# Attention and a gated layer on one core: f16 loads of q and k on GpSimd's queue, more seven-product groups, GpSimd sums, and a fixed order

## The chip, the core and the metric

The kernel runs on 1 core of one Trainium2 chip. A core has TensorE (PE; its weight loads are the row PEld), VectorE (DVE), ScalarE (ACT), GpSimd (POOL) and SyncE (SP), each with an instruction queue that runs in order, and 16 DMA engines that all queues share. The metric is device microseconds of one execution. Three runs of the kernel before took 285.19, 287.29 and 288.51 us; their median, 287.29 us, is the time before.

## The reference, cut to what matters

```python
def phi(x, c, s):                                    # c, s: cos and sin by position
    r = np.maximum(x, 0.0)
    return np.concatenate([r * c, r * s], axis=-1)   # 64 -> 128 features
q_p, k_p = phi(q, cos_w, sin_w), phi(k, cos_w, sin_w)
kv  = np.einsum('bhsf,bhsd->bhfd', k_p, v)
num = np.einsum('bhsf,bhfd->bhsd', q_p, kv)
den = np.einsum('bhsf,bhf->bhs', q_p, k_p.sum(axis=2))[..., None] + 1e-06
x = (num / den).transpose(0, 2, 1, 3).reshape(B * S, H * D)   # 4608 x 512
h = x @ w_in                                                  # 512 x 2048
out = (h * np.cos(h)) @ w_out                                 # 2048 x 512
```

There are 8 batches, 8 heads, 576 positions and 64 features a head. All inputs and the output are float32 in memory.

## The kernel before, in words

**Tiling.** A batch has 576 positions: four tiles of 128 and a rest of 64. The rests of all eight batches make one more block of 512 rows, so the second half of the work (from here on, the layers) runs over nine blocks c = 0 to 8 of 512 rows. Matmul inputs are f16, sums are f32 in PSUM.

**Attention of a batch b.** `load` (L420) brings q, k and v as float32 into the tiles `raw` (named qm, km, vm), two DMAs for each, all issued by SP. `prep` (L443) makes the features: max(x, 0) times cos or sin, 20 instructions of 128x512 for a batch (q and k, five tiles, two halves of the features), on ACT (L452) or DVE (L453). `cast_v` (L457) makes v f16, on DVE, ACT or POOL (L468). `kv` (L471) multiplies and copies the result to `kvz`. q is transposed by a DMA on SP (`q_dma`, L518) or, for batches 0 and 1, by PE. `num` (L527) multiplies q by kv; DVE divides (L566, L568). The result x is transposed by a DMA on SP (`x_dma`, L597) or, for batches 0 to 2, by PE with a copy on ACT (`x_pe`, L581).

**Layer 1.** Blocks 0 and 1 are computed plainly (L637). From block 2 on, the 16 column tiles of w_in are taken in four groups. A group is done in one of two ways. `layer1_plain` (L671), four times for a group, makes 4 matmuls of 128x512 (L677), then `gate` (L606): a cosine on ACT (L609) and a product on DVE (L614). `layer1_fast` (L749) does the group with seven block products instead of eight (Strassen's scheme in Winograd's form): 7 steps of 4 matmuls of 128x256 (L780), with one copy from PSUM to PSUM on ACT (`seed`, L663), two copies to `Z` on ACT (L789), two additions on DVE (L793), two gates, and one double gate `out2` (cosine of 128x1024 on ACT, L802; product on DVE, L808). It needs sums of w_in made once for each group (`w_in_sums`, four instructions on DVE, L717) and, for each block, four sums of x on DVE (`layer1_sums`, L738). `FAST1` says how many groups of a block are done in the seven-product way: 3 in blocks 3 to 6, 4 in blocks 7 and 8, none in block 2.

**Layer 2.** Block 0 is plain (L880). Blocks 1 to 8 use seven products (L948), with sums of w_out made once (L904), four sums of the gated tiles per block on DVE (L926, L979), copies out of PSUM on ACT (L663, L959, L967) and additions on DVE (L963). Two output tiles `ost` are stored by SP.

**What sets the order.** Every step of the kernel is given to a list by `Plan.add`, with its engine or a choice of engines, an estimated cost and the data that it reads and writes. `Plan.run` then walks through a model of the engines (`forward`), picks at each point the ready step with the smallest number in a table `KEYS`, and chooses the engine of a step that has several by the estimated end. The steps are emitted in the order of their modelled start; each engine's queue gets its own in that order. So nothing on the chip is reordered: an instruction that waits holds all behind it on its engine.

**The start.** POOL copies one element of k to w_in's tile as soon as k of batch 0 has landed, and so holds back w_in (four DMAs on POOL, L1033: float32 in memory, f16 in SBUF) and, after w_in's first quarter, the first half of w_out. Batch 1's loads are held back by a copy out of w_in's third quarter (`GATE1`, `hold_raw`, L1052).

Of the kernel before, what the change touches and what calls it, by code (L numbers as in the profile page):

```python
# [17 lines left out]
    5824, 5995, 5824, 2967, 2673, 126, 143, -359, -2881, 263, -1072, -2121, 539, -49, 2962,  # L18
    2726, 3623, 3679, 1739, 3937, 2137, -2208, -6512, 4069, -2017, 702, -6077, -768, 703, -754,
    -6331, 8159, 3076, -1894, -5732, 1581, -6769, -1234, -877, -673, -882, -751, -1585, -1235,  # L20
    617, -63, -2524, -424, -626, 4458, 1519, -1459, -1432, 1518, -1601, 1517, -828, -5827,
    -6392, 1404, 4308, -2500, 2020, -1958, -2107, -3266, -4898, 8136, -5552, -8420, -2791,
    -1468, -4655, -1451, -1052, 783, -6576, 2792, -3465, -355, -8421, -3123, 6479, -3015, -6472,
    -1591, -2075, -2619, -2729, -7369, -6796, 3263, 798, -2481, 6480, -2003, -7073, 6781, 423,
    1982, 1241, 120, -9188, 1380, 643, -11779, -6829, 9984, -8175, -7566, 1246, -8162, 512,
    -312, -11302, 511, 10443, -10259, 2437, 605, 4807, 1897, 5905, -9831, -5057, 9984, 2301,
    -5301, 8846, -10101, -6662, 9020, -11634, -568, 7671, 5055, -1712, 6604, 584, 1196, 5001,
    -1672, 2279, 3129, 2596, 3289, 895, 532, -4417, -5551, -4542, 2044, 1687, 2846, 2800, 1902,
    3378, 993, -5427, 6673, -5442, 8455, 6488, 5906, 5871, 7397, -1850, 7157, -1228, 5182, 5994,
    7349, -880, 4039, 6762, 7533, 1736, 4177, 11737, 11954, 7479, 6368, 6930, 8684, 7392, 5307,  # L30
    17180, 16483, 5398, 7497, -1619, 7409, 8721, -161, 1062, -838, 10292, 5065, 5035, 7002,
    2938, 4999, 14973, 16942, 5320, 7491, 5034, 4630, 11782, 14974, 11886, 4631, 7315, 4601,
    4503, -692, -956, 4504, 7814, 2937, 3132, -860, 16897, -3069, -418, 10427, 3570, 3895, 4526,
    811, 1495, 8147, 4216, 8205, 4347, 7685, 6163, 8521, 4575, 8538, 4733, 3460, 8421, 9350,
    4611, 8493, 5428, 5849, 9131, 9146, 7933, 8134, 4534, 8052, 5570, 6030, 5703, 3236, 9273,
    5079, 7033, 7959, -732, 8555, 4350, -5307, 8046, 8768, 11196, 7765, 7621, 12926, 8253, 8411,
    11956, 11554, 8883, 13897, 9078, 9732, 12216, 1417, 8512, 13854, 7780, 9806, 6177, 5415,
    9049, -520, 5974, 11813, -2437, 5998, 8827, 10404, 7711, 13087, 3521, 9257, 1171, 1138,
    4633, 11805, 2569, 2323, 2261, 2582, 5745, 6182, 8706, 9578, 5077, 10082, 8860, -990, 8453,
    8541, 6221, 8499, 9036, 12232, 10067, 9664, 8544, 14012, 6360, 6188, 8015, 4438, -1489,  # L40
    6985, 8390, 5805, 5879, 5943, 6028, 8049, 8537, 10462, 5198, 8396, 8395, 12558, 4688, 9262,
    6122, 9046, 8189, 3466, 1589, 7820, 11893, 7819, 12664, 3857, 3643, 11985, 9433, 9054, 9210,
    8708, 8410, 9843, 8144, 4689, 8846, 8992, 9753, 8959, 11174, 12280, 10511, 11156, 9526,
    5553, 7072, 10317, 10402, 10261, 8357, 10403, 10051, 10267, 14404, 18351, 12204, 11240,
    9232, 9255, 18421, 14144, 12777, 11783, 7045, 11215, 9090, 7849, 7075, 9381, 10740, 5609,
    9483, 3041, 12189, 10009, 6763, 11687, 7171, 11186, 8968, 9229, 5228, 8069, 10107, 13655,
    8182, 10208, 13199, 8613, 9303, 15205, 7902, 9952, 15535, 6395, 9744, 4204, 6896, 8110,
    15935, 5192, 9656, 15578, 5752, 11091, 9533, 7831, 11765, 13714, 4074, 11936, 4217, 2177,
    4612, 7204, 2638, 7978, 7784, 4545, 8636, 6647, 6639, 5918, 8225, 3758, 5656, 6600, 8239,
    8692, 9382, 5468, 10740, 10372, 5666, 8703, 3916, 8802, 9066, 9050, 9298, 9304, 4801, 9527,  # L50
    9521, 8286, 11521, 9621, 9449, 6022, 5622, 9514, 9669, 10572, 6135, 8767, 7485, 8972, 9413,
    9995, 4213, 8900, 10075, 9675, 10273, 6234, 14794, 10195, 8079, 8885, 4804, 11145, 9576,
    11000, 9480, 10532, 11021, 11980, 10074, 11419, 13188, 13339, 10446, 11020, 12065, 12937,
    12270, 12793, 12994, 13467, 14479, 13933, 13146, 11684, 12054, 13603, 13106, 11695, 11512,
    14005, 13771, 13161, 15965, 16177, 16249, 16753, 13045, 12409, 18114, 13650, 12372, 12951,
    11343, 17252, 18836, 11725, 9919, 9604, 12293, 15415, 7956, 11448, 14519, 12454, 13519,
    14769, 15313, 12053, 13106, 13257, 13105, 13291, 11473, 11759, 13416, 11450, 13716, 18849,
    11925, 12834, 16093, 13478, 14576, 16431, 12255, 12362, 15960, 13160, 14519, 15910, 14407,
    11420, 14173, 9926, 10508, 15133, 9344, 13280, 12367, 9947, 9788, 14407, 10518, 12980,
    11697, 11766, 15535, 11429, 11430, 11395, 14648, 15418, 12373, 10069, 8755, 10521, 8003,  # L60
    11441, 13572, 10404, 12329, 17053, 10754, 11091, 10405, 4849, 9215, 7332, 8545, 10442, 9859,
    10283, 8824, 11855, 11042, 10408, 9428, 9240, 10089, 6840, 10015, 11937, 13432, 12329,
    14986, 8570, 13601, 11278, 9846, 10850, 12123, 10120, 9231, 12906, 11502, 11095, 17486,
    13263, 10990, 10503, 12334, 12434, 12727, 10556, 12848, 11321, 12810, 13349, 12759, 11144,
    9468, 12544, 13893, 13417, 10912, 9663, 12457, 8909, 13137, 14576, 14577, 13435, 14151,
    10310, 14092, 13571, 10884, 9832, 16768, 15657, 11596, 15684, 17182, 16270, 13098, 17070,
    15987, 15606, 6694, 19176, 16271, 6282, 21578, 15029, 12700, 14864, 23503, 25176, 13602,
    15549, 15974, 10832, 14466, 16061, 14589, 10209, 12007, 14031, 13538, 17903, 15093, 14046,
    16754, 11592, 18103, 14972, 15838, 14550, 15534, 14971, 15051, 13097, 12823, 12047, 14361,
    15045, 11016, 15607, 13066, 17291, 15370, 14684, 17730, 15344, 15696, 14507, 15369, 21381,  # L70
    12422, 13612, 16306, 16082, 6980, 15110, 25709, 16196, 6566, 16377, 16411, 13784, 6718,
    14056, 16929, 17039, 16412, 6717, 14282, 13875, 16186, 15098, 22414, 15303, 22094, 16880,
    22547, 17762, 13257, 17979, 16921, 14246, 17264, 11458, 9954, 12478, 12363, 11239, 12491,
# [50 lines left out]


class Plan:


    LINK = {"PE": 0.12, "ACT": 0.05, "DVE": 0.05, "POOL": 0.1, "SP": 0.0}


    SHARE, WAKE, LAND = {"HW": 0.40, "SW": 0.56}, {"HW": 1.1, "SW": 1.3}, 1.0
    BUSY = 2.2

# [48 lines left out]
    def forward(self, key):  # L183
# [32 lines left out]
        for n, k in enumerate(left):  # L216
            if not k:
                ask(n)
# [980 lines left out]
```

## Time and profile before

| | |
|---|---|
| three runs, us | 285.19, 287.29, 288.51 (median 287.29) |
| the profiled execution, us | 284.34 |
| its span, first to last instruction, us | 282.3 |
| around the span, us | 2.04 |
| mean granted clock of TensorE | 0.993 |
| busy, us: PE, PEld, DVE, ACT, POOL | 270.5, 219.1, 249.2, 218.0, 19.2 |

All durations come from this one profiled execution. A row of the profile gives the line, engine and operation, output <- input with partitions x elements, how often it ran, the busy time, the mean duration of one in ns, and the idle time of the engine just ahead of it with what ended it. A "window" row gives the busy time of each engine in a stretch of the span. Instructions of one engine overlap a little: eight matmuls of 128x256 (273 ns each in the row) follow one another in 0.87 us on the chain of waits, four of 128x512 in 0.86 us.

### The profile page before, as it was taken

The page shows a single profiled execution, that of the slowest core. Times are in us where ns is not written, and L with a number is a line of the kernel's source. Part 1 is how long each engine was busy: PE and PEld are TensorE (multiplying, and loading weights), DVE is VectorE, ACT ScalarE, POOL GpSimd, SP SyncE. Part 2 cuts the span into 40 slices and gives each one's busy share as a digit, 9 for nine tenths or more (in the row PEclk, how much of TensorE's full clock was granted, in tenths as well). Part 3 has the DMA queues.
Part 4 walks back from the last instruction along what each step waited for, and adds up shares of the span by engine and source line. Part 5 has one row for each costly group of instructions (what it writes and reads, how often), then busy time and mean ns, then how long its engine had stood idle before and what let it go on. Part 6 is the DMA issues. An engine that isn't in the chain of part 4 may idle for free.

```text
span 282.3 us, 6870 instructions
## 1 busy us (share of the span) xinstructions
PE 270.5 (96%) x2715; PEld 219.1 (78%) x2715; DVE 249.2 (88%) x443; ACT 218.0 (77%) x396; POOL 19.2 (7%) x32
## 2 busy tenths in 40 slices
PE   7799988999989999999999999999999999999994
PEld 2668956678967667779787988898788888888883
DVE  2877796999999989998999999999999999997952
ACT  2856698896899998599899999996676675877420
POOL 1440020010000010003003000210000000000000
PEclk9799999999999999999999999999999999999999
DMA  6999999969979999997999899988013100300124
GB/s 204 312 200 222 298 291 267 320 133 285 311 231 235 211 229 293 241 310 161 308 234 268 167 275 270 240 117 251 3 37 116 57 2 0 151 0 2 74 77 149
DMA packets 77599, 53.30 MB, mean 189 GB/s; under 512 B 46080, under 2 KB 75264, under 8 KB 77568
## 3 DMA queue, kind: packets, MB, share of 16 engines
q1 hardware_dynamic: 72608, 48.12, 66.7%
q0 software_dynamic: 4224, 4.19, 9.5%
q10 hardware_dynamic: 736, 0.57, 0.6%
q8 instruction: 21, 0.34, 0.5%
q14 instruction: 10, 0.08, 0.1%
HBM read 36.74 MB, written 9.44 MB: 164 GB/s over the span
## 4 chain that ended last, share of the span: by engine, by line
PE 85%; DVE 5%; DMA 4%; ACT 3%; issue 1%; DVEq 0%
PE M L948 32%; PE M L780 15%; PE M L637 10%; PE M L677 7%; PE TR L780 6%; PE M L880 5%; PE ATT L542 3%; DMA xT<-x 2%; PE ATT L479 2%; DMA qm<-in_q_dram 2%; PE M L509 2%; PE ATT L1022 1%; PE TR L677 1%; DVE x L568 1%; ACT xT L593 1%; ACT KQ L452 1%
## 5 line engine op out<-in xcount | busy, mean ns | idle before, releaser
L609 ACT ACTIVATE ch<-M 128x512 f32<-128x512 f32 x90 | 53.3, 597 | 14.4 <-PE M L637 6.9
L614 DVE TENSOR_TENSOR gT<-M,ch 128x512 f16<-128x512 f32 x84 | 56.7, 685 | 5.0 <-ACT ch L609 4.6
L948 PEld LDWEIGHTS <-gT 128*128 128x128 f16 x560 | 54.0, 98 | 7.6 <-DVE gT L926 0.5
L948 PE MATMUL M<-w_out_sb,gT 128*128 128x256 f16 x448 | 55.9, 273 | 0.0
L452 ACT ACTIVATE KQ<-km,CS 128x512 f16<-128x512 f32 x55 | 37.2, 715 | 0.2 <-DMA km<-in_k_dram 0.2
L452 ACT ACTIVATE KQ<-qm,CS 128x512 f16<-128x512 f32 x47 | 32.3, 721 | 4.5 <-DMA qm<-in_q_dram 4.5
L780 PEld LDWEIGHTS <-w_in_sb 128*128 128x128 f16 x320 | 30.8, 98 | 4.3 <-issue 0.2
L948 PE MATMUL M<-T,S 128*128 128x256 f16 x256 | 32.4, 273 | 0.0
L637 PE MATMUL M<-xT,w_in_sb 128*128 128x256 f16 x256 | 30.2, 273 | 0.1
L677 PE MATMUL M<-xT,w_in_sb 128*128 128x512 f16 x112 | 27.6, 379 | 0.8 <-ACT xT L593 0.8
L948 PEld LDWEIGHTS <-S 128*128 128x128 f16 x256 | 24.7, 98 | 4.0 <-issue 0.2
L637 PEld LDWEIGHTS <-w_in_sb 128*128 128x128 f16 x256 | 24.5, 98 | 3.5 <-issue 0.4
L568 DVE TENSOR_TENSOR x<-ATT,rec 128x512 f16<-128x512 f32 x32 | 22.1, 692 | 2.3
L959 ACT ACTIVATE ost<-M 128x512 f32<-128x512 f32 x24 | 14.1, 593 | 12.1 <-PE M L948 9.3
L780 PEld LDWEIGHTS <-WS 128*128 128x128 f16 x216 | 20.5, 98 | 3.3 <-issue 0.5
L677 PEld LDWEIGHTS <-w_in_sb 128*128 128x128 f16 x128 | 12.2, 98 | 10.8 <-issue 0.9
L453 DVE TENSOR_SCALAR KQ<-qm,CS 128x512 f16<-128x512 f32 x33 | 15.4, 498 | 5.1 <-DMA qm<-in_q_dram 5.1
L468 POOL CAST V<-vm 128x1024 f16<-128x1024 f32 (+1 forms) x11 | 10.7, 1004 | 134.9 <-PE M L948 46.0
L542 PEld LDWEIGHTS <-qT 128*128 128x128 f16 x320 | 15.3, 98 | 4.6 <-issue 1.8
L926 DVE TENSOR_TENSOR S<-gT 128x2048 f16<-128x2048 f16 (+1 forms) x16 | 17.4, 1085 | 0.2
L808 DVE TENSOR_TENSOR gT<-Z,ch 128x1024 f16<-128x1024 f32 x13 | 15.9, 1221 | 0.7 <-ACT ch L802 0.4
L542 PE MATMUL ATT<-kvz,qT 128*128 128x65 f16 x288 | 15.7, 194 | 0.6 <-DVE x L568 0.5
(135 smaller groups left out, 461.3 us busy)
## 6 DMA issues: line engine op xcount, KB each, us to landing
out_dram<-ost SPq DMA_DIRECT2D x33, 256.0 KB, 3.0
qm<-in_q_dram SPq DMA_DIRECT2D x8, 640.0 KB, 5.9
km<-in_k_dram SPq DMA_DIRECT2D x8, 640.0 KB, 5.6
qm<-in_q_dram SPq DMA_DIRECT2D x8, 512.0 KB, 6.2
km<-in_k_dram SPq DMA_DIRECT2D x8, 512.0 KB, 5.7
vm<-in_v_dram SPq DMA_DIRECT2D x6, 640.0 KB, 7.2
vm<-in_v_dram SPq DMA_DIRECT2D x6, 512.0 KB, 6.5
w_in_sb<-in_moe_w_in_dram POOLq DMA_DIRECT2D x4, 512.0 KB, 8.9
```

The lines of the kernel that those rows point to most:

```text
L452: fn = {"ACT": lambda: nc.scalar.activation(out=out_, in_=in_, func=AF.Relu, scale=sc), "DVE": lambda: nc.vector.tensor_scalar(out=out_, i ...
L453: "DVE": lambda: nc.vector.tensor_scalar(out=out_, in0=in_, scalar1=0.0, scalar2=sc, op0=ALU.max, op1=ALU.mult)}
L542: nc.tensor.matmul(bank[hb][:, hh * D1:(hh + 1) * D1], lhsT=a[:, h, :], rhs=z[:, h, :], start=(i == 0), stop=(i == len(parts) - 1))
L568: nc.vector.tensor_tensor(out=split(x16[n][:, hs, :], k), in0=A[:, :, :, 0:D], in1=split(rec[n][:, hs], k).unsqueeze(3).broadcast_to((P, k ...
L609: act(0.5, due, lambda: nc.scalar.activation(out=ch[c], in_=bank, func=AF.Sin, bias=math.pi / 2.0, scale=1.0), [key], [("ch", c)])
L614: dve(0.61, due, lambda: nc.vector.tensor_tensor(out=dst, in0=a, in1=b, op=ALU.mult), [key, ("ch", c), *rd], dkeys)
L637: nc.tensor.matmul(M1[m][:, jj * 2 * P:(jj + 1) * 2 * P], lhsT=w_in_sb[:, cc, j * P:(j + 1) * P], rhs=X[:, cc, ts], start=(cc == 0), stop= ...
L677: nc.tensor.matmul(M, lhsT=w_in_sb[:, cc, j * P:(j + 1) * P], rhs=X[:, cc, :], start=(cc == 0), stop=(cc == NCT - 1))
L780: nc.tensor.matmul(bank[0][:, j * TH:(j + 1) * TH], lhsT=a(cc, j), rhs=b[:, cc, :], start=(first and j == 0 and cc == 0), stop=(last and j ...
L808: dve(1.14, due, lambda: nc.vector.tensor_tensor(out=g4, in0=four(uz), in1=four(cc2), op=ALU.mult), zk + ck, [("g", gi(c), h * JH + j, t) ...
L926: dve(0.07 + 1.07 / NG, due, lambda: nc.vector.tensor_tensor(out=out_[:, sl], in0=a[:, sl], in1=b[:, sl], op=op), rd, wr, port=True)
L948: nc.tensor.matmul(bank[0][:, tt * MH:(tt + 1) * MH], lhsT=a[:, j, tt * P:(tt + 1) * P], rhs=b[:, j, :], start=(first and (apart or tt == ...
```

## The change

- `load`: q and k of batches 2 to 7 go to new f16 tiles `R16`, one for q and one for k (`NK = 1`), by DMAs that POOL issues; float32 in memory, f16 in SBUF. v, and batches 0 and 1, stay as they were. `prep` of those batches reads f16. `clear16` clears the unused rest of the two tiles once, on POOL.
- `FAST1`: all four groups in blocks 2 to 8, that is 28 groups in place of 20. `OWN = 4`: all four groups' sums of w_in have tiles of their own (the fourth used q's transposed tiles before).
- `sums`: the sums of w_in, of x, of the gated tiles and of w_out, and the product of `out2`, may run on DVE or POOL. `copies`: the copies out of PSUM may run on ACT or DVE.
- The float32 tiles of q and k share their memory with the tiles T2 to T4, S2 and S3 of layer 2; the sums that write those wait for batch 1's features. The spare tiles of the last two blocks move to R16, vm and V1.
- Batch 1's loads are held back by w_in's first quarter in place of the third.
- `Plan.run` models nothing any more: an entry of `KEYS` divided by ten is the place of the step in the order, and its last digit names the option (0: only one; 1, 2, 3: first, second, third engine in the order in which the code lists them). There are 1461 entries in place of 1407.

```diff
     def run(self):
         st = self.steps
         assert len(KEYS) == len(st)
-        start, done = self.forward([k / 100 for k in KEYS])
-        for s, a, b in zip(st, start, done):
-            s["start"], s["end"] = a, b
-        return sorted(st, key=lambda s: (s["start"], s["n"]))
...
+        for s, k in zip(st, KEYS):
+            self.pick(s, k % 10)
+            s["at"] = k // 10
+        assert all(st[d]["at"] < s["at"] for s in st for d in s["deps"])
+        return sorted(st, key=lambda s: (s["at"], s["n"]))
+
+    def pick(self, s, i):
+        if i:
+            e = list(s["opts"])[i - 1]
+            s["opts"] = {e: s["opts"][e]}
             s.update(zip(("eng", "occ", "lat", "fn"), s["opts"][e]))
...
-    T2, T3, T4 = [sb(f"T{n}", [P, JH, MH]) for n in range(2, 5)]
-    S2, S3 = [sb(f"S{n}", [P, JH, TH]) for n in (2, 3)]
-    raw = {nm: sb(f"{nm}m", [P, H, NT + 1, D], F32) for nm in "kqv"}
+    TS = sb("TS", [P, 5 * JH * MH])
+    T2, T3, T4, S2, S3 = [TS[:, n * JH * MH:(n + 1) * JH * MH].rearrange("p (j m) -> p j m", j=JH)
+                          for n in range(5)]
+    raw = {nm: TS[:, 2 * n * RAW:2 * (n + 1) * RAW].bitcast(F32).rearrange(
+        "p (h t d) -> p h t d", h=H, t=NT + 1) for n, nm in enumerate("kq")}
+    raw["v"] = sb("vm", [P, H, NT + 1, D], F32)
+    NK = 1
+    R16 = {nm: sb(f"{nm}h", [P, NK, H, NT + 1, D]) for nm in "kq"}
...
-    GATE1 = (w_in_sb[0:2, 0, Dff // 2 + 1:Dff // 2 + 2], [("w_in", 2)])
+    GATE1 = (w_in_sb[0:2, 0, 1:2], [("w_in", 0)])
...
+    def copies(due, cost, out_, in_, rd, wr, hint):
+        either(due, cost, {
+            "ACT": lambda: nc.scalar.activation(out=out_, in_=in_, func=AF.Copy),
+            "DVE": lambda: nc.vector.tensor_copy(out=out_, in_=in_)}, rd, wr, hint, port=False)
+
+    def sums(due, n, out_, in0, in1, op, rd, wr, lazy=None, rate=0.523e-3):
+        def go(q):
+            return lambda: q.tensor_tensor(out=out_, in0=in0, in1=in1, op=op)
+        either(due, {"DVE": 0.07 + n * rate, "POOL": 0.05 + n * 2.15e-3},
+               {"DVE": go(nc.vector), "POOL": go(nc.gpsimd)}, rd, wr, 1, lazy=lazy)
...
     def load(b, nm, due, hs=(slice(0, H),)):
-        m, n = raw[nm], b % 2
+        (m, key), n = staged(b, nm), b % 2
+        cast = m.dtype == F16
+        q = nc.gpsimd if cast else nc.sync
...
+    def clear16():
+        for nm in "kq":
+            pl.add("POOL", 1.2, 1.35, 22, lambda nm=nm: nc.gpsimd.memset(R16[nm][:, :, :, NT, :], 0.0), [],
+                   [x for n in range(NK) for x in hk(f"{nm}h{n}")], port=True)
...
-        out_, in_ = dst[:, t, hs, g, :], raw[nm][:, hs, t, :]
+        m, key = staged(b, nm)
+        out_, in_ = dst[:, t, hs, g, :], m[:, hs, t, :]
...
-        act(0.5, due, lambda: nc.scalar.activation(out=dst[0], in_=bank[0], func=AF.Copy),
-            [bank[1]], [dst[1]])
+        copies(due, {"ACT": 0.5, "DVE": 0.61}, dst[0], bank[0], [bank[1]], [dst[1]], 1)
...
-    FAST1 = {3: 3, 4: 3, 5: 3, 6: 3, 7: 4, 8: 4}
-    CH2, OWN = NCT // 2, 3
+    FAST1 = {2: 4, 3: 4, 4: 4, 5: 4, 6: 4, 7: 4, 8: 4}
+    CH2, OWN = NCT // 2, 4
...
-        tt(T3, b22, b12, ALU.subtract, wk, ["T3"])
+        tt(T3, b22, b12, ALU.subtract, wk, ["T3"] + hk("k") + hk("q"))
...
     first_attention()
+    clear16()
     layer1(0)
```

## The prediction

> **What bounds the kernel now.** I read the page's busy times first, then the windows by stage, the chain of waits, the waits by pair, the groups, and the landing times of the loads.
>
> ```profile
> PE 270.5 (96%) x2715; PEld 219.1 (78%) x2715; DVE 249.2 (88%) x443; ACT 218.0 (77%) x396; POOL 19.2 (7%) x32
> PE 85%; DVE 5%; DMA 4%; ACT 3%; issue 1%; DVEq 0%
> ```
> ```profile
> 20.00:78.00 58.00, 56.01 (x602) 44.13 (x603) 50.52 (x102) 48.01 (x90) 3.42 (x8) 1.00 1.04 265
> 78.00:84.00 6.00, 5.25 (x39) 3.44 (x37) 5.86 (x11) 5.99 (x12) 0.00 (x0) 1.00 0.71 219
> 84.00:194.00 110.00, 109.15 (x1166) 88.49 (x1165) 105.32 (x187) 101.45 (x186) 9.60 (x10) 1.00 1.07 239
> 194.00:264.00 70.00, 70.00 (x648) 61.09 (x647) 66.33 (x102) 47.11 (x83) 0.00 (x0) 1.00 0.15 49
> 264.00:282.30 18.30, 14.19 (x131) 12.47 (x128) 9.70 (x15) 5.11 (x8) 0.00 (x0) 0.98 0.31 116
> ```
> ```profile
> 79.92 0.50 ACT xT L593
> 80.45 2.75 PE M L677 x12
> ...
> 99.36 6.57 DMA xT<-x
> 106.03 0.74 DVE XS L738
> ```
>
> In a window row the columns are stretch, PE, PEld, DVE, ACT and POOL busy, granted clock, DMA share, GB/s. TensorE bounds the kernel: 85% of the chain is its own work, and from 84 to 264 us it lacks 0.85 us of 180. Its idle time after the first 20 us is 1.99 us up to 78, 0.75 us in the next six (the first products of block 2 wait for x's copy on ACT), 0.85 us up to 194 (the sums of x for block 3 wait for x's transposes) and 4.1 us behind the last matmul. From 84 to 194 us DVE has only 4.7 us free and ACT 8.5 us: there the cushion is thin.
>
> ```profile
> L609 ACT ACTIVATE ch<-M 128x512 f32<-128x512 f32 x90 | 53.3, 597 | 14.4 <-PE M L637 6.9
> L614 DVE TENSOR_TENSOR gT<-M,ch 128x512 f16<-128x512 f32 x84 | 56.7, 685 | 5.0 <-ACT ch L609 4.6
> L452 ACT ACTIVATE KQ<-km,CS 128x512 f16<-128x512 f32 x55 | 37.2, 715 | 0.2 <-DMA km<-in_k_dram 0.2
> L453 DVE TENSOR_SCALAR KQ<-qm,CS 128x512 f16<-128x512 f32 x33 | 15.4, 498 | 5.1 <-DMA qm<-in_q_dram 5.1
> L468 POOL CAST V<-vm 128x1024 f16<-128x1024 f32 (+1 forms) x11 | 10.7, 1004 | 134.9 <-PE M L948 46.0
> km<-in_k_dram SPq DMA_DIRECT2D x8, 640.0 KB, 5.6
> w_in_sb<-in_moe_w_in_dram POOLq DMA_DIRECT2D x4, 512.0 KB, 8.9
> ```
>
> The reader should see here the price of a feature step on ACT (0.72 us) and on DVE (0.48 us, the median by line), and that the kernel already has f16-casting loads on GpSimd's queue: w_in's.
>
> **The change, part by part.**
>
> *Seven-product groups.* FAST1 goes from 20 groups to 28: four more in block 2, one more in each of blocks 3 to 6. A plain group is 16 matmuls of 128x512, 4 in 0.86 us on the chain: 3.44 us. A fast one is 28 of 128x256, 8 in 0.87 us: 3.05 us. Eight groups take 8 x 0.39 = 3.1 us off TensorE, all of it on the path that sets the end. Each group costs ACT four cosines less (-2.39), one seed, two copies, two cosines (5 x 0.597) and one double cosine (1.055): +1.65 us. It costs DVE two gates less (-1.37), two additions (+1.36) and a double product (+1.22): +1.2 us. Together ACT +13.2, DVE +9.7.
>
> *Where the steps run* (counted by the last digits of the new table). GpSimd gets 10 double products, 10 sums of w_in, 13 sums of x and 3 sums of layer 2: 36 new tensor instructions. DVE loses 12.2 + 4.2 + 3.1 us for the first, second and fourth; of the sums of x there are 28 for 24, 15 on DVE: -3.8 us. No row shows a two-input GpSimd instruction. Lower bound: the casts' time (1.09 us for 1024 elements, 0.63 for 512), 31 us in all; upper, twice that, since two inputs are read: 62 us. I take 62, the row being of one input. ACT's features of batches 2 to 7 fall from 85 to 66 (-13.6 us), DVE's rise from 35 to 54. What an f16 one costs on DVE is not shown: at most 0.478 as now; at least 0.39, since a 128x256 cast, with the same input bytes, takes 0.333 us where a 128x512 one takes 0.420. I take 0.39: 54 x 0.39 - 35 x 0.478 = +4.4 us (+9.1 at the upper end). Twenty copies move from ACT to DVE: 16 x 0.69 + 4 x 0.42 = +12.8 us there, -12.0 on ACT. Casts: about -1 on DVE, +2 on ACT; ACT also gets 5 more of den, +0.9. Sums: DVE +9.7 - 12.2 - 4.2 - 3.8 - 3.1 + 4.4 + 12.8 - 1.0 = +2.6 us, of 33 us idle over the span; ACT -9.5 us. TensorE's work beside them covers both; without that cover the 2.6 us would be on the path.
>
> *Loads.* 24 DMAs leave SP (0.65 us each, 15.6 us) for POOL (0.86 us each as w_in's, 20.6 us). They no longer stand among the transposes of q and x on SP; there they now stand among sums on POOL. GpSimd's total is about 19 + 62 + 21 = 102 us: far from a bound. The 6.57 us wait for x's transposes above was on SP's queue, with v and k loads between them: half of the 0.85 us behind it I take as won (0 to 0.85).
>
> *Block 2.* Its four sums of x now stand ahead of the third product. In the table one x transpose's copy is followed on PE by two steps of layer 2 (1.74 us) and two first products (0.87), where the plain block waited: the 0.75 us goes (0 to 0.75). All 16 sums of w_in come before it; 10 on GpSimd, 6 on DVE (2.5 us), beside layer 1 of block 1.
>
> *Other edits.* The two clears on GpSimd (0.53 us by the row of its 128x512 fill, L1008) lie at 17 to 30 us, between w_in's and w_out's DMAs, where POOL idles; uncovered, 1.1 us. Sharing memory makes T3, S2 and S3 wait for batch 1's features, made before 50 us, 15 us ahead of their use. GATE1 lets k of batch 1 go when w_in's first quarter has landed (17.6 us) in place of 20.7, and the table puts q and v behind them; the idle 1.99 us there I leave.
>
> *Sum* against the profiled execution (284.34 us = span 282.3 + 2.04): -3.1 (products), -0.7 (block 2), -0.4 (transposes), +0.3 for new waits of that sort = -3.9, 280.4 us. That execution lies 2.95 us under the median of the three runs, so for a median I say 287.3 - 3.9 = 283.4 us.
>
> **Two rules that speak against it.** The trace shows DVE held beside GpSimd's casts: a sum of x took 745 ns for 416, two features 767 and 612 for 478, 0.75 us of waiting beside 10.9 us of casts. The Trainium skill ("SBUF — State Buffer", Who interferes with whom) says why: a GpSimd instruction that reads SBUF and a DVE one with two SBUF inputs or in a two-port mode exclude each other for the whole instruction; the trace agrees, and what it would do to the sum is the first rival. The second row is the issue of w_in's loads: 792 to 923 ns each while DVE ran four features back to back. The same page (A bandwidth-pool intuition that's wrong) has a GpSimd-issued DMA go from 620 to about 3100 ns beside a DVE copy, as its descriptors can't be written; these rows don't show it, and the third rival prices it.
>
> **The rivals.**
>
> 1. *The lock eats the gain.* From 84 to 194 us about 18 of the new GpSimd instructions run, 5 x 2.2 + 12 x 1.25 + 4.4 = 30 us. At the rate seen (0.07 us of waiting per us) DVE waits 2.1 us more: inside its 4.7 us. If each holds DVE for half its length, 15 us: 10 us too many. It decides from 0.16 per us on. For it: two in five DVE instructions are of the held kind. Against it: products from PSUM, the others, are not seen held. At 0.3 per us, 9.0 - 4.7 = +4.3 on top of -3.9: 287.7 us. Features no faster in f16 (+4.7 us on DVE) end at the same place.
>
> 2. *More idle time goes.* All 0.85 + 0.75 + 1.99 us: -3.1 - 3.6 = -6.7, 280.6 us. For it: no load stands on SP ahead of a transpose but v's. Against it: the 1.99 us lies in batch 1's attention, which keeps its form.
>
> 3. *Slower: the loads land late.* There is one f16 tile for q and one for k, so a batch's load waits on POOL until the features of the batch before are made. In the table the PE steps between the issue of k's second load and its first feature make 8.1, 6.4, 6.4, 6.8 and 6.9 us for batches 3 to 7 (mean 6.9). k's loads on SP land in 5.6 us (median; up to 13.4), w_in's on POOL in 6.2 to 12.0, median 8.9, four at once. The features stand at the head of DVE's and ACT's queues, with every gate behind them. DVE's free time is 4.7/110 x 27 = 1.15 us a batch. Landing in 8 us, as two in flight suggest, is covered; at 8.9 us it costs 5 x 0.85 = 4.2, the whole gain; at 10 us 5 x 1.95 = 9.8: 284.34 + 9.8 - 3.9 + 2.95 = 293.1 us. It decides from 9 us on.
>
> That the groups don't save TensorE time is excluded by the two rates above, both in this trace.
>
> **How the numbers follow.** Forecast 0.5 (283.4; its own range 281.5 to 285.5 by the two halves that I took), rival 1 0.2, rival 2 0.1, rival 3 0.2. A measurement tells 1% here: under 284.4 is faster, over 290.2 slower. Faster: 0.40 of the forecast's half, 0.1 of rival 2, 0.04 of rival 1: 0.54. Slower: 0.15 of rival 3 and 0.01 of rival 1: 0.16. Same: 0.30. The range leaves out half of rival 3 and the edges of the others: 280.0 to 291.0.
>
> **What would show it.** Right: L677 gone, L780 with 784 matmuls, PE's busy time some 3 us less; window 84 to 194 as full as before; no wait for the f16 tiles among the longest. Wrong by rival 1: sums of x, features or gated sums on DVE far over their rows, ahead of idle PE. By rival 3: ACT and DVE waiting for q's or k's DMA beyond 20 us, in every batch. Wrong on sizes: features in f16 at 0.48 us, or a double product on GpSimd far from 2.2 us.

## The result, and the profile after

| | kernel before | changed kernel |
|---|---|---|
| median of four runs | 287.25 us (285.19 to 288.51) | 299.7 us (295.88 to 301.12) |
| profiled execution; its span | 284.34; 282.3 us | 299.63; 297.8 us |
| ratio | | 1.040 (95% interval 1.030 to 1.050) |
| TensorE busy; idle from 20 us to its last matmul | 270.5; 3.6 us | 272.5; 18.0 us |

The change made the kernel 4% slower; 283.4 us was forecast, with a range up to 291.0. Executions of one kernel fall into a faster group and, now and then, a slower one by some per cent: ratios and intervals, here and below, are taken from the faster ones, medians and ranges from all. The same views as before, first busy times, granted clock and DMA queues from the page (the clock line has a digit for each 7.4 us, in tenths, 9 standing for 90% or more):

```profile
PE 272.5 (92%) x2811; PEld 229.1 (77%) x2811; DVE 254.5 (85%) x450; ACT 212.4 (71%) x381; POOL 100.3 (34%) x94
...
PEclk9999999999779999999999999999999999999999
...
q1 hardware_dynamic: 59936, 33.96, 50.1%
q0 software_dynamic: 16896, 11.27, 27.6%
```

Then windows (stretch, PE, PEld, DVE, ACT and POOL busy, granted clock, DMA share, GB/s):

```profile
20.00:78.00 58.00, 52.41 (x556) 40.84 (x555) 50.63 (x103) 44.74 (x84) 18.24 (x24) 1.00 1.20 235
70.00:84.00 14.00, 9.33 (x77) 6.96 (x76) 11.62 (x19) 7.37 (x15) 5.48 (x6) 0.82 1.29 222
84.00:99.00 15.00, 13.61 (x152) 11.88 (x151) 13.36 (x21) 12.03 (x21) 5.67 (x5) 0.94 0.39 79
84.00:194.00 110.00, 99.83 (x1109) 87.07 (x1108) 99.25 (x168) 91.79 (x168) 39.10 (x35) 0.99 0.99 164
194.00:264.00 70.00, 69.92 (x703) 62.71 (x702) 63.35 (x101) 51.11 (x88) 30.22 (x15) 1.00 0.30 72
```

And TensorE's waits between 20 and 180 us (engine, tile, line, what it waited for: us in total, times, longest):

```profile
PE ATT L471 <- DVE x L497: 7.9, 4, 4.7
PE M L872 <- ACT ost L328: 3.1, 2, 2.6
PE M L707 <- ACT Z L328: 2.2, 2, 2.1
PE M L806 <- DMA w_out_sb<-in_moe_w_out_dram: 1.7, 1, 1.7
PE M L707 <- DVE gT L540: 1.4, 1, 1.4
```

The reader should see where the loss lies. The last blocks (194 to 264 us), in which nothing is loaded any more, are as full as before, 69.92 of 70 us. From 84 to 194 us TensorE has 10.2 us idle where it had 0.85, and up to 78 us it has 5.6 where it had 2.0. The difference of the spans, 15.5 us, is 14.4 us more idle time after the first 20 us, 0.9 less before, and 2.0 us more of busy TensorE. That last term holds the 3.1 us saved by the new groups and about 5 lost: at the lower clock of two of the windows, 9.33 x 0.18 + 13.61 x 0.06 = 2.5 us by the rows, and the rest isn't placed. From 84 to 194 us ACT and DVE aren't busier than before (91.8 us for 101.5, and 99.3 for 105.3): they stand waiting, too. What they wait for shows in the timeline of DVE, then of GpSimd, then of TensorE, around the longest of these waits (start, duration, engine, line, work; in brackets its idle time and what ended that):

```profile
75.48 3.61 DVE L386 TENSOR_SCALAR KQ<-kh,CS 128x512 f16<-128x512 f16 x1 [1.89 <-DMA kh<-in_k_dram]
79.01 0.19 DVE L495 RECIPROCAL rec<-den 128x8 f32<-128x8 f32 x1
79.30 0.69 DVE L497 TENSOR_TENSOR x<-ATT,rec 128x512 f16<-128x512 f32 x1
```
```profile
74.12 0.73 POOL L356 DMA_DIRECT2D qh<-in_q_dram  x1 [3.45 <-DVE KQ L386]
74.85 0.70 POOL L359 DMA_DIRECT2D qh<-in_q_dram  x1
75.54 2.28 POOL L333 TENSOR_TENSOR w_in_sb<-w_in_sb 128x512 f16<-128x512 f16 x2
77.77 1.16 POOL L333 TENSOR_TENSOR WS<-w_in_sb,WS 128x512 f16<-128x512 f16 x1
```
```profile
80.14 0.60 PE L471 MATMUL ATT<-kvz,qT 128*128 128x65 f16 x8 [4.67 <-DVE x L497]
```

One f16 feature of k on DVE, 0.346 us by the median, takes 3.61 us: it starts as the first of three GpSimd sums does (two are in the row at 75.54) and ends with the last. Ahead of it DVE had already waited 1.89 us for k of batch 3 to land. Behind it stands the division L497, and behind that TensorE, 4.67 us idle, with its clock at 0.82 over the window around it (70 to 84 us). So both mechanisms of the slower rivals are there, one in front of the other: GpSimd's sums hold DVE, and k lands late.

### The profile page after: what moved, and what is told of

Same layout as the page of the kernel before. It is cut to its first block, busy times and chain, and to the rows that moved or that the text cites. A ratio compares the mean times of both kernels' runs of the same rounds, so it can differ in the third digit from the quotient of the medians.

```text
span 297.8 us, 7159 instructions
## 1 busy us (share of the span) xinstructions
PE 272.5 (92%) x2811; PEld 229.1 (77%) x2811; DVE 254.5 (85%) x450; ACT 212.4 (71%) x381; POOL 100.3 (34%) x94
## 3 DMA queue, kind: packets, MB, share of 16 engines
q1 hardware_dynamic: 59936, 33.96, 50.1%
q0 software_dynamic: 16896, 11.27, 27.6%
## 5 line engine op out<-in xcount | busy, mean ns | idle before, releaser
L535 ACT ACTIVATE ch<-M 128x512 f32<-128x512 f32 x74 | 43.4, 594 | 12.1 <-PE M L563 7.2
L872 PE MATMUL M<-TS 128*128 128x256 f16 x256 | 32.4, 273 | 2.6 <-ACT ost L328 2.6
L563 PE MATMUL M<-xT,w_in_sb 128*128 128x256 f16 x256 | 30.6, 277 | 0.3 <-ACT xT L328 0.3
L333 POOL TENSOR_TENSOR gT<-Z,ch 128x1024 f16<-128x1024 f32 x7 | 17.0, 2431 | 41.0 <-ACT ch L729 23.4
L872 PEld LDWEIGHTS <-TS 128*128 128x128 f16 x256 | 24.8, 98 | 5.8 <-issue 2.8
L385 ACT ACTIVATE KQ<-kh,CS 128x512 f16<-128x512 f16 x35 | 24.3, 716 | 5.2 <-DMA kh<-in_k_dram 5.2
L729 ACT ACTIVATE ch<-Z 128x1024 f32<-128x1024 f32 x22 | 23.3, 1058 | 5.1 <-DVE Z L720 5.0
L720 DVE TENSOR_TENSOR Z<-M,Z 128x512 f32<-128x512 f32 x34 | 22.8, 685 | 2.9 <-ACT Z L328 2.0
L471 PEld LDWEIGHTS <-qT 128*128 128x128 f16 x320 | 15.4, 99 | 12.0 <-issue 10.5
L385 ACT ACTIVATE KQ<-qh,CS 128x512 f16<-128x512 f16 x31 | 21.9, 721 | 3.5 <-issue 3.5
L497 DVE TENSOR_TENSOR x<-ATT,rec 128x512 f16<-128x512 f32 x32 | 22.1, 692 | 2.3
L328 ACT ACTIVATE Z<-M 128x512 f32<-128x512 f32 x34 | 19.8, 595 | 5.3 <-PE M L707 3.4
L707 PE MATMUL M<-XS,w_in_sb 128*128 128x256 f16 x144 | 21.4, 272 | 1.6 <-DVE gT L540 1.4
L707 PE MATMUL M<-xT,w_in_sb 128*128 128x256 f16 x144 | 21.6, 272 | 0.0
```

Source lines behind the costliest of these rows:

```text
L328: "ACT": lambda: nc.scalar.activation(out=out_, in_=in_, func=AF.Copy),
L333: return lambda: q.tensor_tensor(out=out_, in0=in0, in1=in1, op=op)
L385: fn = {"ACT": lambda: nc.scalar.activation(out=out_, in_=in_, func=AF.Relu, scale=sc), "DVE": lambda: nc.vector.tensor_scalar(out=out_, i ...
L471: nc.tensor.matmul(bank[hb][:, hh * D1:(hh + 1) * D1], lhsT=a[:, h, :], rhs=z[:, h, :], start=(i == 0), stop=(i == len(parts) - 1))
L497: nc.vector.tensor_tensor(out=split(x16[n][:, hs, :], k), in0=A[:, :, :, 0:D], in1=split(rec[n][:, hs], k).unsqueeze(3).broadcast_to((P, k ...
L535: act(0.5, due, lambda: nc.scalar.activation(out=ch[c], in_=bank, func=AF.Sin, bias=math.pi / 2.0, scale=1.0), [key], [("ch", c)])
```

## The experiments

The theories: **lock** (GpSimd's sums and casts hold DVE instructions), **late loads** (the f16 loads land after their turn), **start** (k of batch 1 ahead of w_out), and, of the lock, whether it costs in proportion to GpSimd's work or by runs and places. Each kernel is the changed one with the edit shown; each time is a median, and the ratio is to the kernel before on the same chip. There that took 284.0 to 286.6 us, beside the changed kernel 287.25; so times of different runs can't simply be subtracted, and gains are read from the ratios, where a hundredth is 2.9 us. The changed kernel's 1.040 is known to a hundredth either way, and so no gain against it better than to some 3 us. Where more is needed, TensorE's idle time in the profiled executions helps, from 20 us to its last matmul: 3.6 us before, 18.0 in the changed kernel.

**Taking the suspects out.** The sums on GpSimd cut short:

```diff
...
+        w = out_.shape[-1] // 16
+        o_, a_, b_ = [ap[..., 0:w] for ap in (out_, in0, in1)]
-               {"DVE": go(nc.vector), "POOL": go(nc.gpsimd)}, rd, wr, 1, lazy=lazy)
+               {"DVE": go(nc.vector), "POOL": lambda: nc.gpsimd.tensor_tensor(
+                   out=o_, in0=a_, in1=b_, op=op)}, rd, wr, 1, lazy=lazy)
...
```

> The changed kernel, but the 36 two-input sums that the table puts on GpSimd work on one sixteenth of their columns; the cosines' bias is 0.5 and the scratch tiles are filled with zeros on DVE at the start, so the values are not the reference's, while every instruction on TensorE, ACT and DVE keeps its size and its place. GpSimd's v casts and loads stay. Theory LOCK (GpSimd's sums hold DVE while they run; the feature at 75.5 us took 3.61 us for 0.35 beside three of them, the layer-2 sum at 93.4 us 2.99 for 1.22): the 4.67 us and 1.39 us idle of TensorE behind them go, about 6.5 us of waiting in all, and with the long idle the clock drop behind it (0.82 and 0.94 granted, about 3.4 us): 299.7 - 6.5 - 3.4 = 290 us. Theory LATE LOADS (the q and k loads on GpSimd's queue land late and hold the features at the heads of ACT and DVE): only the load that stood behind sums (second q load of batch 6, 4 us after the first) comes earlier, worth 1.6 us: 298 us.

Measured 290.2 us (288.0 to 296.5; ratio 1.009, 1.003 to 1.016). The lock was worth about what its theory said: 3.1 hundredths, some 9 us, with TensorE's idle time down to 5.9 us. The zeros at the start stood in the way of an exact sum, as they held the first loads (5.0 us wait for the first feature, 0.9 in the changed kernel). The loads cut short:

```diff
+            if cast and b > 2:
+                h = slice(0, 1)
+                five, four = five[:, h], four[:, h]
```

> The changed kernel, but the f16 loads of q and k of batches 3 to 7 carry one head of eight (80 and 64 KB of source data in place of 640 and 512); the features then work on old data in the other heads. Their issues on GpSimd stay. LATE LOADS: each of them lands in under 4 us in place of 4.2 to 14.5, and the waits that I put down to them go (about 7.6 us: part of the 4.67 at 80 us, 2.08 + 0.50 at 125 us, 2.64 at 134 us, 1.6 at 163 us): 292 us, less if the clock drop behind the 4.67 us goes as well (289). LOCK: the waits stay but for 1 to 2 us that were the loads' traffic: 298 us.

Measured 291.9 us (291.2 to 292.1; ratio 1.017, 1.015 to 1.020). The late loads are a cause too, 2.3 hundredths or some 6.5 us, with 9.4 us idle. Both edits together:

> Both of the cuts before in one kernel (sums on GpSimd at one sixteenth, f16 loads of batches 3 to 7 at one head). If LOCK and LATE LOADS together hold the loss: 299.7 - 6.5 - 7.6 - 3.4 = 282 us, with w_out's 1.7 us at 37 us left, and 28 seven-product groups then show their 3.1 us less of TensorE work. If it stays over 288 us, a third cause is at work (copies and sums moved between ACT and DVE by the table, or the order itself).

Measured 285.3 us (285.1 to 285.5; ratio 0.995). No third cause of that size is left; 4.0 us are idle. With the zeros moved behind the clears:

> Sums on GpSimd at one sixteenth of their columns, f16 loads of batches 3 to 7 at one head of eight and bias 0.5 as before (values not the reference's), but the zeros for the scratch tiles come behind the three clears of the raw tiles, so that the first loads are not held (TensorE waited 4.85 us for the first feature there, 0.9 us in the changed kernel). What is left is then the change without its two costs: 285.3 - 2.7 (the later second q load) = 282.6 us, 4 us under the kernel before, by which the 3.1 us of the seven-product groups would be there. If it stays at 285 us, the later start was hidden, and the groups give less than 3.1 us.

Measured 282.06 us (281.8 to 282.3; ratio 0.992, 0.989 to 0.995), with these busy times and windows:

```profile
PE 267.6 (96%) x2811; PEld 227.0 (81%) x2811; DVE 251.2 (90%) x458; ACT 211.8 (76%) x381; POOL 46.7 (17%) x94
```
```profile
20.00:78.00 58.00, 55.17 (x595) 43.56 (x594) 52.71 (x113) 47.03 (x90) 12.43 (x23) 1.00 1.12 225
84.00:194.00 110.00, 108.11 (x1252) 96.28 (x1250) 106.66 (x188) 99.84 (x183) 21.77 (x40) 1.00 0.77 156
```

TensorE is busy for 267.6 us here, 2.9 less than before: the eight groups' 3.1 us are real. TensorE's idle time is 4.7 us. Without the two costs the change would have won 0.8%, and what they cost is 1.040 - 0.992 = 4.8 hundredths, some 14 us (299.7 - 282.1 = 17.6 us between the medians as they stand, of which 287.25 - 284.6 = 2.6 us is the chips). The fourth cell, with only the sums cut:

> GpSimd's 36 sums at one sixteenth of their columns, bias 0.5 (values not the reference's), loads whole, and the zeros for the scratch tiles behind the clears of the raw tiles, so that the start is not held. With the changed kernel (299.7), short loads alone (291.9) and both short (282.1) this fills the fourth cell. If the two costs are independent, sums alone are worth what they are worth beside short loads, 291.9 - 282.1 = 9.8 us: 289.9. If each makes the other worse, both single steps give more than their share: 290.2 - 2.7 (the start) = 287.5 us.

Its executions took 286.5 us and 291.3 to 292.7 us. The four cells (ratio; idle time in the profiled execution):

| | loads whole | loads short |
|---|---|---|
| sums whole | 1.040; 18.0 us | 1.017; 9.4 us |
| sums short | 1.009 to 1.030; 7.8 us | 0.992; 4.7 us |

By the times the fourth cell isn't settled: lock alone is worth between one and three hundredths, 3 to 9 us, loads alone some 6.5, and whether they just add stays open. The idle times speak for an overlap: 10.2 us less without the lock and 8.6 without the late loads, but 13.3 and not 18.8 without both, as one stands in front of the other at 80 us. The 7.8 us are from this cell's fastest execution, though.

**The start.** One line back:

```diff
-    GATE1 = (w_in_sb[0:2, 0, 1:2], [("w_in", 0)])
+    GATE1 = (w_in_sb[0:2, 0, Dff // 2 + 1:Dff // 2 + 2], [("w_in", 2)])
```

> The changed kernel with one line as it was: k of batch 1 waits for w_in's third quarter again, not for its first. Theory START ORDER: k then no longer loads beside w_in's last quarters and ahead of w_out's first half; the 1.69 us that layer 2 of block 0 waits for w_out at 37 us go, 298.0 us. Rival: k's features and with them block 1's attention come later by about 3 us of landing, and a wait of 1 to 2 us at 43 to 48 us takes its place (the kernel before had 1.20 us at 43 us): 299.7 us.

Measured 300.6 us (ratio 1.050, 1.045 to 1.055); the wait for w_out is still 1.72 us, at 38.5 us. The start theory falls: that gate isn't what delays w_out.

**Sums given back to DVE**, by kind, each in its old place of the order:

```diff
-               {"DVE": go(nc.vector), "POOL": go(nc.gpsimd)}, rd, wr, 1, lazy=lazy)
+               {"DVE": go(nc.vector), "POOL": go(nc.vector if lazy else nc.gpsimd)}, rd, wr, 1, lazy=lazy)
```

> The changed kernel with only the 10 sums of w_in that ran on GpSimd (eleven us of work there, in runs of two and three) back on DVE, in the same places of the order: +4.2 us of DVE work. LOCK IN RUNS (what hurts is several GpSimd instructions back to back, which keep one DVE instruction waiting to the end of the last): the 3.61 us feature at 75.5 us and the 2.99 us sum at 93.4 us go, 3.3 + 1.8 + 0.4 us of DVE waiting, and the clock drop: 291 to 293 us. LOCK IN PROPORTION (every us of GpSimd's two-input sums costs DVE the same): these are 12 of 96 us, so about 1.5 us, and the added 4.2 us on DVE eat that: 299 us.

Measured 295.6 us (its executions: 291.5, 293.0, 298.3 and 299.5; ratio 1.025, 1.016 to 1.034, from the first two, which are where the lock in runs put them). With `rate > 0.001` for `lazy`, the double products:

> The changed kernel with only the 10 double products that ran on GpSimd (2.4 us each up to 169 us, 4 to 5 us later, 36 to 45 us in all) back on DVE, in the same places: +12.2 us of DVE work. LOCK IN RUNS: in the trace only one of them stood beside a lengthened DVE instruction (0.89 us at 160.9 us), so there is nothing to win but that, and DVE, with some 3 to 5 us free a block, gets more to do: 299 to 303 us. LOCK IN PROPORTION: they are 40% of GpSimd's sums, 4 to 5 us come back: 295 us.

Measured 300.2 us (297.3 to 301.0; ratio 1.051). Twelve us of GpSimd's work were worth some 4, and 24 of it nothing (the double products took 2.4 us throughout, not the 4 to 5 that I wrote). That speaks for the lock in runs and not in proportion, but it doesn't settle it alone, since the second edit puts 12.2 us on DVE and the first 4.2. The traces are plainer: the wait of 4.67 us is still there, of the same length, with the double products on DVE, and 0.46 us of it is left with w_in's sums there. With `True`, all 36:

> The changed kernel with all 36 sums on DVE, none on GpSimd, the order unchanged: +25.6 us of DVE work (10 x 1.22 + 23 x 0.42 + 3 x 1.22), 245 + 26 = 271 us in all. LOCK: the waiting goes as in the kernel with the sums cut short (290 us), but DVE is now as busy as TensorE, so that it lands between: 290 to 297 us. LATE LOADS: the lock was not the matter, and DVE's work adds: over 300 us.

Measured 299.2 us (296.8 to 302.3; ratio 1.047), above the range of the lock's theory, and no gain: with no sum on GpSimd DVE's 267.5 us of work stand in the way instead, with six waits of 0.47 to 1.30 us on TensorE from 194 us on, where the changed kernel has none over 0.25. So GpSimd's help can't simply be dropped; it is a matter of which sums, and where.

**Why the loads land late.** The waits behind late loads that stand apart from the sums begin with k of batch 5 (ACT, then TensorE, in the changed kernel):

```profile
123.35 0.72 ACT L385 ACTIVATE KQ<-kh,CS 128x512 f16<-128x512 f16 x1 [3.08 <-DMA kh<-in_k_dram]
124.60 0.60 PE L707 MATMUL M<-XS,WS 128*128 128x256 f16 x4 [2.08 <-ACT Z L328]
```

Leaving out 25 of q's 30 DMA transposes:

```diff
-        pl.add("SP", 1.25, 0, due, lambda: nc.sync.dma_start(
+        pl.add("SP", 1.25, 0, due, lambda: b > 2 or nc.sync.dma_start(
```

> The changed kernel without the DMA transposes of q of batches 3 to 7 (25 of the 30 on SP's queue); the products of q with kv use batch 2's. SHARED RINGS (the f16 loads land late because they share the DMA engines with these transposes): q of batch 5 lands in 6 to 8 us in place of 12.7 and 14.5, k of batches 3 and 5 in 5 to 7; the waits at 125 to 135 us (5.2 us) go, and part of the others: 293 to 295 us. ONE TILE / ORDER (they are issued too late, since each waits for its only tile and stands behind sums): landing shortens little, the time stays at 297 to 300 us.

Measured 292.5 us (291.8 to 294.1; ratio 1.030, 1.025 to 1.034), a hundredth less, which is no more than 1.040 itself is known to. The trace says more. The time from issue to landing of q's twelve f16 loads, in the changed kernel and in this one:

```profile
DMA to landing us min/median/max: 4.7/6.8/14.5
```
```profile
DMA to landing us min/median/max: 4.4/5.3/7.6
```

Batch 5's two q loads land in 5.4 and 5.5 us in place of 14.5 and 12.7, the waits from 124 to 135 us (5.2 us) are gone, and TensorE's idle time is 12.1 us for 18.0. Before, loads and transposes stood behind each other on SP's queue; now they are on two queues and move at the same time. That isn't all of the lateness: k of batch 3 lands in 10.5 us here too (10.4 in the changed kernel), and the 4.67 us behind it stay 4.66. The two loads of v, which SP issues beside it at 64.4 and 65.1 us, may be what it meets, or the cast itself may slow it; neither was tried. Loads delay transposes as well: q's land in 5.6 us in the changed kernel, 4.8 before (medians). Moving k's loads ahead, with k in two tiles, was no gain in any of three kernels:

```diff
...
-            s["at"] = k // 10
+            s["at"] = MOVED.get(s["n"], k // 10)
...
-    NK = 1
-    R16 = {nm: sb(f"{nm}h", [P, NK, H, NT + 1, D]) for nm in "kq"}
+    NKS = {"k": 2, "q": 1}
+    R16 = {nm: sb(f"{nm}h", [P, NKS[nm], H, NT + 1, D]) for nm in "kq"}
...
```

MOVED gives a step, by its number, another place in the table's order (hundredths of a us): here k's ten loads of batches 3 to 7 and two of q's.

> The changed kernel with two f16 tiles for k (five KB more in each partition), so that k's loads wait for nothing but the clear: those of batches 3 to 7 stand 6 to 9 us earlier in GpSimd's order, and the second q loads of batches 5 and 6 directly behind the first, ahead of the sums that held them back. Nothing is left out. LATE LOADS: k of batches 3 and 5 has landed when its features' turn comes, which takes away the 2.15 and 3.08 us of waiting on ACT and the 1.6 us at 163 us; q of batch 5 (landing in 13 to 14 us beside the transposes) may stay: 294 to 296 us. LOCK ALONE: no gain, 299 us.

Measured 298.2 us (295.6 to 298.4; ratio 1.044): no gain, where 294 to 296 us were expected. With w_in's sums on DVE as well:

> Two of the edits together, nothing left out: the 10 sums of w_in on DVE, and k in two f16 tiles with its loads 6 to 9 us earlier. With k two tiles alone one DVE feature was held 4.96 us behind four GpSimd sums of w_in in a row, so the loads' part could not show. If LOCK IN RUNS and LATE LOADS are both causes, they add: 295.6 - 3 to 5 for k's loads = 291 to 293 us. If the loads' lateness is only the other face of the lock, it stays with the sums of w_in alone: 295 us.

Measured 298.4 us (296.8 to 303.3; ratio 1.048), worse than with w_in's sums alone. And with v's casts on ACT in addition:

```diff
-              "POOL": lambda: nc.gpsimd.tensor_copy(out=out_, in_=in_)}
+              "POOL": lambda: nc.scalar.activation(out=out_, in_=in_, func=AF.Copy)}
```

> The kernel with those two edits, and v's casts that ran on GpSimd (11, of 0.6 to 2 us) on ACT in the same places: +9 us on ACT, which is 71% busy. LOCK: DVE features and sums held by casts (0.88 + 0.78 us at 106 us, 0.65 at 141 us, 0.42 at 169 us; 0.95 and 0.80 us with k in two tiles) are let go: 1 to 2 us less than without. RIVAL: ACT's added 0.9 us stand in front of the copies and cosines that TensorE waits for: 1 to 3 us more.

Measured 311.5 us (303.4 to 312.9), far worse than either theory said, and why is open. In the profiled execution TensorE's longest wait, 3.92 us at 222 us, stands behind a DVE double product that took 5.08 us for 1.22 beside a GpSimd sum of 4.05: a hold in a new place. What ACT's casts cost by themselves isn't known.

**Order and place.** First, the colliding instructions taken off GpSimd (sums of w_in, one double product, three sums of x) and two q loads moved:

```diff
+MOVED = {819: 10245, 986: 12730}
...
+ON_DVE = (375, 367, 368, 369, 372, 376, 370, 377, 381, 382, 448, 741, 742, 743)
...
-            self.pick(s, k % 10)
+            self.pick(s, 1 if s["n"] in ON_DVE else k % 10)
...
```

> Nothing left out. All 16 sums of w_in on DVE, the double product of block 2's second group and block 4's three sums of x too (the GpSimd instructions that held DVE over 0.3 us in the runs so far), and the second q loads of batches 5 and 6 directly behind the first; 22 sums stay on GpSimd; +6.7 us of DVE work. LOCK IN RUNS with LATE LOADS: under the kernel with only the sums of w_in on DVE (295.6) by the 2.08 us behind the double product and the 1 to 2 us of late second q loads: 291 to 293 us; the rest of the loads' cost stays, since they still share the rings with the transposes. RIVAL (every change of the order opens other waits, as with k's loads moved): 295 us or more.

Measured 291.5 us (289.5 to 295.1; ratio 1.022, 1.018 to 1.026): the time that was expected, but beside the 1.025 with only w_in's sums on DVE no gain that can be told. Then no step on another engine, six sums ahead of batch 4's loads:

```diff
+MOVED = {370: 6750, 372: 6740, 376: 7030, 377: 7050, 381: 8245, 382: 8250,
+         819: 10245, 986: 12730}
...
```

> Nothing left out, no step changes its engine: six of GpSimd's sums of w_in stand ahead of the loads of batch 4 (q's two, then k's two) and not behind them, and the second q loads of batches 5 and 6 stand directly behind the first. BUNCHING (in the changed kernel the sums pile up behind a load that waits for its only tile, and then run back to back under DVE's features): the 3.61 us feature and the 2.99 us sum go: 292 to 295 us. RIVAL (the six sums now run back to back earlier, from about 68 to 75 us, under the features of batch 3's q, and hold those): 298 to 301 us.

Measured 289.1 us (286.9 to 291.5; ratio 1.015, 1.010 to 1.021), better than both of its theories: 2.5 hundredths, some 7 of the 14 us, back for eight numbers of the table. DVE and GpSimd in this kernel, around the same place:

```profile
72.38 3.63 DVE L396 TENSOR_SCALAR KQ<-qh,CS 128x512 f16<-128x512 f16 x3
75.94 0.34 DVE L396 TENSOR_SCALAR KQ<-kh,CS 128x512 f16<-128x512 f16 x1
```
```profile
71.34 2.13 POOL L343 TENSOR_TENSOR WS<-w_in_sb,WS 128x512 f16<-128x512 f16 x1
73.43 1.20 POOL L343 TENSOR_TENSOR w_in_sb<-w_in_sb 128x512 f16<-128x512 f16 x1
74.72 1.15 POOL L343 TENSOR_TENSOR WS<-w_in_sb 128x512 f16<-128x512 f16 x1
```

The sums hold DVE here too: three features of q take 3.63 us for 1.04. But they do so while k is still on its way (it lands at 75.41 us), when DVE would have waited anyway, and k's feature then takes its 0.34 us. Over the whole kernel DVE's instructions are lengthened by 10.3 us against the medians of their kinds, in the changed kernel by 10.6: there is as much holding as before. What fell is TensorE's idle time, 18.0 to 10.4 us, and in two ways that weren't measured apart. The waits from 124 to 135 us (5.2 us) are gone, since q of batch 5 lands in 7.2 and 8.4 us in place of 14.5 and 12.7; this goes with the two moved q loads. And the 4.67 us at 80 us are 2.26, and those of 1.39, 1.09 and 1.58 us are gone, while one of 4.50 us is new, behind a sum of x that took 3.65 us at 111.66 beside a double product; this goes with the places of the sums. Two trials to go on from there. The first gives DVE the double product that held a sum of x in this kernel:

```diff
+ON_DVE = (484,)
...
```

> The kernel with the order changed (six sums of w_in and two q loads moved ahead, 289.1 us), and the one GpSimd instruction in it that still cost TensorE a long wait moved to DVE: the double product of block 2's last group, which kept a sum of x for 3.65 us (0.42 us otherwise), with 4.50 us of idle TensorE behind it. Nothing is left out. PLACE (what counts is which DVE instruction is held, not how much holding there is): 289.1 - 4.5 + 1.2 at most = 284.6 to 286 us, level with the kernel before. RIVAL (another hold or a late load takes its place at 117 us, block 3's first product waiting for its features all the same): 288 to 290 us.

Measured 289.1 us (288.2 to 294.6; ratio 1.012, 1.005 to 1.018): no gain that can be told, as the rival had it. The 3.65 us sum of x is gone, but k and q of batch 5 now land in up to 9.6 and 13.2 us, and three waits of 1.37, 0.97 and 0.50 us take the place of the one of 4.50.

With two tiles for k in addition, and `488: 5410, 489: 5405`:

> The same, and k in two f16 tiles with the loads of batch 3 alone moved, directly behind those of its q (about 57 us in place of 64 us). PLACE and LATE LOADS: k of batch 3 lands near 68 us, not 72 to 75, and the 2.26 us that TensorE waits at 77 us go: 283 to 284 us, at or under the kernel before. RIVAL (as when all of k's loads were moved: the earlier load meets the transposes of q of batch 2 and holds v's and q's behind it): 286 to 290 us.

Measured 294.8 us (293.3 to 301.3; ratio 1.032). k of batch 3 does land at 69.4 us, but its chain of waits between 66 and 77 us is:

```profile
ACT KQ L400 <- DMA qT<-KQ: 3.7, 1, 3.7
DVE gT L555 <- ACT ch L550: 3.1, 1, 3.1
...
PE M L578 <- DVE gT L555: 2.8, 1, 2.8
```

Two transposes of q take 8.58 us on SP's queue beside the loads (a transpose takes 1.28 us there by the median of the changed kernel); q's next features may not overwrite KQ before, and ACT, DVE and TensorE wait in turn. No version beat the kernel before; the two at 289.1 us (1.015 and 1.012) are the best that compute everything.

## Why the prediction was wrong, point by point

The step that failed is the cover. The sum put the 36 GpSimd sums and the 24 moved loads at nothing on TensorE's path (DVE's total and "TensorE's work beside them covers both", GpSimd's 102 us "far from a bound"), and the loads even at a gain of 0.4 us. The runs put these two at 4.8 hundredths, some 14 us: with both costs the ratio is 1.040, without them 0.992, and TensorE's idle time 18.0 and 4.7 us. The rest of the sum held in the main: of the 1.4% that it forecast (283.4 of 287.3 us), 0.8% is won without these costs.

- *TensorE bounds the kernel; seven-product groups, -3.1 us.* Right: 2.9 us less busy time with both costs out, and 194 to 264 us stayed full.
- *Block 2, -0.7 us.* Right as a mechanism: with both costs out no wait stands at 80 us. In the changed kernel the 4.67 us stand there, from the attention ahead of it.
- *Transposes, -0.4 us, since loads no longer stand among them on SP.* Wrong in sign. Taking the loads off SP's queue let them run beside the transposes. x's do land sooner (3.5 us for 4.4, medians), but q's land later (5.6 for 4.8) and loads up to 14.5 us: with q's left out 5.2 us of waits are gone, and 5.9 us of idle time, where short loads take away 8.6. So what I priced as a gain was a good part of the loads' cost; k of batch 3 is late without these transposes too.
- *Prices of instructions.* Close: double product on GpSimd 2.43 us (2.2 taken), small sums 1.16 (1.25), GpSimd in all 100.3 us (102), ACT 212.4 (208.5). The f16 feature on DVE was cheaper than both my bounds, 0.346 us for 0.39 to 0.478. DVE's 254.5 us, 2.7 above the sum's 251.8, hold 10.6 us of lengthening.
- *Start, idle time left as it is.* Of little weight: 1.69 us for w_out at 37 us are new, 1.2 us of another wait at 43 us went.
- *Rival 1 (the lock), 0.2.* The mechanism came, and my measure for it failed. I counted waiting per us of GpSimd's work against DVE's free time, with 0.16 as the point from which it decides. In the stretch that I counted for, 84 to 194 us, it was 5.8 us of lengthening in 29.8 us of sums and casts, 0.20. That is over the point, but by my sum worth only 5.8 - 4.7 = 1.1 us, and the lock cost 3 to 9. The longest hold lay ahead of that stretch, at 75.5 us. A free share over a block is no cushion for one 3.3 us hold at the head of a queue. The Trainium skill ("SBUF — State Buffer", Who interferes with whom), as I used it, lets whoever issues first keep the shared pair for the whole instruction. The trace agrees where one cast holds a feature for about its own length (1.23 us at 106.18, beside a cast of 1.05 at 106.22), though by the recorded starts the feature was the earlier; but three sums in a row kept one feature for all three, and four did for 4.96 us in the kernel with two k tiles.
- *Rival 3 (late loads), 0.2.* Came as well. I put the turning point at a landing of 9 us, and medians were 6.6 us for k and 6.8 for q, so by that rule it should have been covered. The tail did it, of loads that a feature waited for: k of batch 3 in 10.4, of batch 5 in 9.4, q of batch 5 in 14.5 us. The rule named beside this rival, of the Trainium skill ("SBUF — State Buffer", A bandwidth-pool intuition that's wrong), by which a DMA issued by GpSimd waits while a DVE copy keeps its descriptors from being written, isn't what delayed them: GpSimd's issues took 0.69 to 0.75 us for k, with DVE 85% busy.
- *How the numbers follow.* The rivals were given chances as if only one could come. By the trace from 74 to 79 us they are linked: a load that waits for its only tile stops GpSimd's queue, the sums behind it bunch up, and they run just when the features that wait for the other load start. Both came, the two cost some 14 us by the ratios where the larger of the two was given 9.8, and the range ended 8.7 us short.

What I named as signs, features on DVE far over their rows ahead of idle PE, and ACT and DVE waiting for k's and q's DMA beyond 20 us, is what the trace shows. I expected the latter in every batch; it is batches 3, 5 and 6.

## What to carry to other kernels

A wait per unit of work, or a median landing time, says little about an engine that works in order: ask which instruction stands at the head when the longest hold or the latest load falls, and what is queued behind it. When transfers leave a queue, look at what they will now run beside, and not only at what they no longer stand behind. Before work is taken off a shared engine, try its place in the order: eight entries of a table, six for sums and two for loads, were worth 2.5 hundredths of the time here, some 7 us, and moving all 36 sums to DVE nothing (1.047 for 1.040).

## What the runs showed of the hardware

- GpSimd instructions back to back can keep a DVE feature out from the first to the last (3.61 us for three, 4.96 for four), yet in another order (the table with eight entries moved) three features in a row were kept for about one sum each (1.24, 1.24 and 1.30 us; a GpSimd sum takes 1.15). GpSimd is held as well: its sum at 71.34 us there took 2.13 us, beside a two-input DVE sum of 1.28 us that had begun at 71.18. What decides between a hold of one sum and of several wasn't tried.
- f16 loads that cast take longer on the DMA engines than the f32 loads which they replace, though they write half the bytes. The same 12,672 packets went from one queue to the other: q1's time fell by 66.7% of 282.3 - 50.1% of 297.8 = 39 us, q0's rose by 27.6% of 297.8 - 9.5% of 282.3 = 55 us, 1.4 times as much, some of it perhaps from running beside others.
- The granted clock fell behind long idle times of TensorE, but not by their length alone. Behind the 4.67 us it was 0.57 from 78 to 86 us. It fell behind 2.26 us in the kernel with eight entries moved (0.57 from 78 to 82 us) and behind 2.81 us in the last kernel (0.79 from 72 to 80 us), and stayed at 1.00 behind 2.27 us in the one before the last (74 to 83 us), behind 2.64 us in the changed kernel (130 to 140 us) and behind 3.11 us in the one with the colliding instructions taken off (142 to 150 us). The Trainium skill ("TensorE: Matmul & The Clock Gate", Part 1) gives about 3.4 us as the idle window. The 4.67 us agrees with that, the falls behind 2.26 and 2.81 us don't.
